# Writing a decode block's output in two halves: two column tiles, one PSUM bank, one copy and one eight-row transfer each

## The chip, the cores and the metric

The kernel runs on one core of one Trainium2 chip. The metric is the device time of one execution in microseconds (us), as the median of several runs. One further execution was taken with the profiler; its rows are what is read here.

## What is computed

One token for each of four sequences (B = 4, D = 512) passes a layer norm. The normalised row feeds an attention block and a gated feed-forward block, and both results are added to the row itself:

```python
xn = _layernorm(x)                                  # x: [4, 1, 512] bf16
q  = xn @ wq                                        # 32 heads of 128
k, v = the last W = 4096 positions of the caches    # 8 key/value heads, 4 query heads to each
a  = softmax(q k^T * 128**-0.5) v                   # per head
A  = a.reshape(4, 1, 4096) @ wo                     # [4096, 512]
Bf = (silu(xn @ w_gate) * (xn @ w_up)) @ w_down     # F = 1792
out = x + A + Bf                                    # [4, 1, 512] bf16
```

All inputs and the output are bf16. The output has four rows of 512 elements, 1 KB each.

## The kernel before

**Staging.** All large loads are put on SP's queue in one order: `wq`, `w_gate`, `w_up`, then keys and values of the eight key/value heads (4 MB each, two buffers each), `w_down`, and at the end `wo` in four pieces of 22, 5, 3 and 2 of its 32 row blocks (`WOS`, `load_wo`, line 257). `wo` takes the place of a key buffer. Loads of keys and values wait for the buffer to come free (`s_tr`, `s_pv`).

**Main loop.** For each of the eight heads TensorE (PE) transposes the keys, VectorE (DVE) and ScalarE (ACT) copy the transposes out of PSUM, PE forms the scores, DVE takes maxima, ACT the exponentials, and PE multiplies by the values. GpSimd (POOL) only builds constants at the start: memsets, then selections that write identity-like patterns, two semaphores (`s_go`, `s_const`) between them.

**The end, around the change.** The normalised attention output of the last head is permuted by PE into `perm_ps`, and DVE writes it to `OP` (line 374), of whose 32 columns per row block four (one per sequence) hold data and the rest are zero. `guT`, the feed-forward's hidden row, has the same layout (line 368). Two accumulators collect the output:

- `acc4` (line 478): one product of 32 x 512 for each row block, in bank `ps_S[1]`. Row block t goes to column tile t % 4 of the array, so that the four tiles hold four partial sums of the full 512 columns, at partitions 0, 32, 64 and 96. It takes all of `w_down` (14 blocks) and the first 22 blocks of `wo`.
- `acc` (line 482): for each row block four products of 4 x 128, one for each quarter of the output columns, quarter n in column tile n. All four lie in bank `ps_S[0]`, quarter n at partitions 32n to 32n+3. It starts with `x` itself (through an identity) and takes the last ten blocks of `wo`.

When `acc4` is complete (`s_e`), ACT copies it to `S2` in SBUF (line 292), and four fp32 products with the selector `sel4` add its four partial sums into `acc`, between the second and the third piece of `wo`. The last two blocks of `wo` wait for its fourth piece (`d_wo[3]`); the last product of all signals `s_acc`.

**The output.** On `s_acc` DVE copies quarters 0 and 1 from PSUM to `y` (line 377, two copies of 4 x 128), and ACT quarters 2 and 3 (line 295, two copies). `y` is a tile of 4 partitions x 512. Each half of the columns then goes out in one transfer of four rows of 512 bytes: the first on SP's queue (line 269, on `s_y[0]`), the second on ACT's (line 298, on `s_y[1]`). SP ends the kernel when both have landed (`d_out` at 32).

Of the kernel before, what the change touches and what calls it, by code (L numbers as in the profile page):

```python
# [3 lines left out]
BF16 = mybir.dt.bfloat16  # L4
FP32 = mybir.dt.float32
# [5 lines left out]
def bass_parallel_sum__sliding_block_cached__swiglu_ffn__decode_kernel(  # L11
# [39 lines left out]
    def sb(name, shape, dtype, align=32):  # L51
        return nc.alloc_sbuf_tensor(name, shape, dtype, align_bytes=align)
# [33 lines left out]
    on = sb("on", [128, NH], FP32)  # L86
    OT = sb("oT", [128, B, HKV, REP, 4], BF16)

    OP = sb("oP", [128, NR, 32], BF16)
    S2 = sb("s2", [128, D], FP32)  # L90
    sel4 = sb("sel4", [128, B], FP32)
    ex = sb("ex", [128, NF, B], FP32)
    gs = sb("gs", [128, NF, B], FP32)
    guT = sb("guT", [128, NF, 32], BF16)
# [8 lines left out]
    dr = sb("dr", [128, NR], BF16)  # L103
    sel = sb("sel", [128, 32], FP32)
    head = sb("head", [128, 128], FP32)
    y = sb("y_sb", [B, D], BF16)

    ps = nc.alloc_psum_tensor
    ps_kt = [ps("ps_kt%d" % s, [128, 512], FP32) for s in range(3)]
# [14 lines left out]
    up_ps = ps_O[:, 128:128 + NF * B]  # L124
    xT_ps = ps_S[2][:, 0:NC * B]
    HD = D // 4
    acc_ps = ps_S[0][:, 0:HD]
    acc4_ps = ps_S[1]
    perm_ps = ps_kt[2][:, 0:B * NR]

# [42 lines left out]
    s_y = [sem("s_y%d" % n) for n in range(2)]  # L173

    x_ap = A_x.rearrange("b s d -> (b s) d")
    out_ap = out.rearrange("b s (n c) -> n (b s) c", n=2)
    wq_ap = A_wq.rearrange("(p c) n -> p c n", c=NC)
    wg_ap = B_w_gate.rearrange("(p c) n -> p c n", c=NC)
    wu_ap = B_w_up.rearrange("(p c) n -> p c n", c=NC)
# [6 lines left out]
    def on_gpsimd(eng):  # L186
        eng.memset(ident[:], 0.0)
        eng.memset(I4[:], 0.0)
        eng.memset(ones[:], 1.0)
        eng.memset(own[:], 1.0)  # L190
        eng.memset(moff[:], 0.0)
        eng.memset(coff[:], 0.0)
        eng.memset(neg[:], 0.0)
        eng.memset(dq[:], 1.0)
        eng.memset(dr[:], 0.0)
        eng.memset(sel4[:], 0.0)
        eng.memset(guT[:].rearrange("p t b -> p (t b)"), 0.0)
        eng.memset(OP[:].rearrange("p t b -> p (t b)"), 0.0)
        eng.memset(sel[:], 0.0)
        eng.memset(head[:], 0.0)  # L200
        eng.memset(CM[:], 0.0)
        eng.memset(QT[:, HKV, :], 0.0)
        eng.drain().then_inc(s_go, 1)

        def select(t, pattern, op, fill, base, mult):
            eng.affine_select(t, t, pattern=pattern, compare_op=op, fill=fill, base=base,
                              channel_multiplier=mult)
        select(I4[:], [[-1, B]], ALU.not_equal, 1.0, 0, 1)
        select(ident[:], [[-1, 128]], ALU.not_equal, 1.0, 0, 1)
        select(neg[:], [[-1, NH]], ALU.not_equal, -1.0, 0, 1)  # L210
        ownv = own[:].rearrange("k (j b) -> k j b", b=B)
        moffv = moff[:].rearrange("k (j b) -> k j b", b=B)
        coffv = coff[:].rearrange("k (b h) -> k b h", h=REP)
        select(ownv, [[0, NJ], [-REP, B]], ALU.is_ge, 0.0, 0, 1)
        select(moffv, [[0, NJ], [-REP, B]], ALU.is_ge, OFF, 0, 1)
        select(coffv, [[-REP, B], [0, REP]], ALU.is_ge, OFF, 0, 1)
        select(dq[:], [[-32, 4]], ALU.is_ge, 0.0, 0, 1)
        select(dr[:], [[-1, NR]], ALU.not_equal, 1.0, 0, 1)
        eng.drain()
        select(ownv, [[0, NJ], [REP, B]], ALU.is_ge, 0.0, REP - 1, -1)  # L220
        select(moffv, [[0, NJ], [REP, B]], ALU.is_ge, OFF, REP - 1, -1)
        select(coffv, [[REP, B], [0, REP]], ALU.is_ge, OFF, REP - 1, -1)
        select(dq[:], [[32, 4]], ALU.is_ge, 0.0, 31, -1)
        for a in range(1, 4):
            eng.drain()
            select(dr[:], [[-1, NR]], ALU.not_equal, 1.0, -32 * a, 1)
        eng.drain().then_inc(s_const, 1)

        for n in range(4):
            select(sel[:], [[-1, 32]], ALU.not_equal, 1.0, -32 * n, 1)  # L230
            select(head[:], [[0, 128]], ALU.not_equal, 1.0, -32 * n, 1)
            select(sel4[:], [[-1, B]], ALU.not_equal, 1.0, -32 * n, 1)
            eng.drain()
        eng.memset(dsum[:], 0.0)
        eng.memset(Osb[:], 0.0)
        eng.drain().then_inc(s_zero, 1)

    def on_sync(eng):
        def load(g):
            u = g % 2  # L240
            if g >= 2:
                eng.wait_ge(s_tr, NCH * (g - 1))
            if g < HKV - 1:
                eng.dma_start(KB[u][:], kv_ap(A_k_cache, g, 0, NT)).then_inc(d_k[u], 16)
            else:

                H = NT // 2
                eng.dma_start(KB[u][:, 0:H], kv_ap(A_k_cache, g, 0, H)).then_inc(d_k[u], 16)
                eng.dma_start(KB[u][:, H:], kv_ap(A_k_cache, g, H, NT)).then_inc(d_kh, 16)
            if g == 1:  # L250
                eng.wait_ge(s_q, 1)
            if g >= 2:
                eng.wait_ge(s_pv, g - 1)
            eng.dma_start(VB[u], kv_ap(A_v_cache, g, 0, NT)).then_inc(d_v[u], 16)

        def load_wo(n, a, b):
            eng.dma_start(WO[:, a:b, :], wo_ap[:, a:b, :]).then_inc(d_wo[n], 16)  # L257

        eng.dma_start(WQ, wq_ap).then_inc(d_wq, 16)
        eng.dma_start(WG[:], wg_ap).then_inc(d_wg, 16)  # L260
        eng.dma_start(WU[:], wu_ap).then_inc(d_wu, 16)
        for g in range(HKV):
            load(g)
        eng.dma_start(WD[:], wd_ap).then_inc(d_wd, 16)
        eng.wait_ge(s_tr, NCH * (HKV - 1))
        for q in range(4):
            load_wo(q, WOS[q], WOS[q + 1])
        eng.wait_ge(s_y[0], 1)
        eng.dma_start(out_ap[0], y[:, 0:D // 2]).then_inc(d_out, 16)
        eng.wait_ge(d_out, 32)  # L270

    def on_scalar(eng):
        eng.wait_ge(s_go, 1)
        eng.dma_start(X[:], x_ap).then_inc(d_x, 16)
        eng.wait_ge(s_var, 1)
        eng.activation(st_std[:], st_var[:], ACT.Sqrt).then_inc(s_std, 1)

        def group(r):
            for n, c in enumerate(ACT_CH):
                eng.wait_ge(s_tr, r * NCH + (c + 1))  # L280
                eng.activation(KT[:, c % 4], kt_ps[c % 3], ACT.Copy).then_inc(s_ea, 1)  # L281
            for q in range(NB):
                eng.wait_ge(s_mk, r * NB + (q + 1))
                eng.activation(P[:, BT * q:BT * (q + 1), :], ps_S[q][:].rearrange("p (t n) -> p t n", n=NH),  # L284
                               ACT.Exp, scale=SCALE).then_inc(s_p, 1)

        eng.wait_ge(s_gu, 1)
        eng.activation(ex[:], gate_ps.rearrange("p (t b) -> p t b", b=B), ACT.Exp, scale=-1.0).then_inc(s_ex, 1)
        with eng.Fori(0, HKV) as r:
            group(r)  # L290
        eng.wait_ge(s_e, 1)
        eng.activation(S2[:], acc4_ps[:], ACT.Copy).then_inc(s_ec, 1)
        eng.wait_ge(s_acc, 1)
        for n in range(2, 4):
            last = eng.activation(y[:, HD * n:HD * (n + 1)], acc_ps[32 * n:32 * n + B, :], ACT.Copy)
        last.then_inc(s_y[1], 1)
        eng.wait_ge(s_y[1], 1)
        eng.dma_start(out_ap[1], y[:, D // 2:D]).then_inc(d_out, 16)

    def on_vector(eng):  # L300
        eng.wait_ge(d_x, 16)
# [63 lines left out]
        eng.drain()  # L365
        eng.tensor_tensor(gs[:], gate_ps.rearrange("p (t b) -> p t b", b=B), ex[:], ALU.mult)
        eng.drain()
        eng.tensor_tensor(guT[:, :, 0:B], up_ps.rearrange("p (t b) -> p t b", b=B), gs[:], ALU.mult).then_inc(s_guT, 1)
        group(0)
        with eng.Fori(1, HKV) as r:  # L370
            group(r, lambda: norm(r - 1))
        norm(HKV - 1)
        eng.wait_ge(s_pm, 1)
        eng.tensor_copy(OP[:, :, 0:B].rearrange("p r b -> p b r"), perm_ps.rearrange("p (b r) -> p b r", b=B)).then_inc(s_pc, 1)
        eng.wait_ge(s_acc, 1)
        for n in range(2):
            last = eng.tensor_copy(y[:, HD * n:HD * (n + 1)], acc_ps[32 * n:32 * n + B, :])  # L377
        last.then_inc(s_y[0], 1)

    def on_tensor(eng):  # L380
        mm = eng.matmul
# [95 lines left out]
        def acc4(n, left, right, start, stop):  # L477
            return mm(acc4_ps[32 * n:32 * n + 32, :], left, right, start=start, stop=stop, skip_group_check=True)

        def acc(left, right, start, stop):  # L480
            for n in range(4):
                last = mm(acc_ps[32 * n:32 * n + B, :], left, right[:, HD * n:HD * (n + 1)],
                          start=start, stop=stop, skip_group_check=True)
            return last

# [38 lines left out]
            last = mm(perm_ps[:, NR * b:NR * (b + 1)], OT[:, b].rearrange("p k h q -> p (k h q)"), dr[:])  # L524
        last.then_inc(s_pm, 1)
        spin(2, 1)
        acc(ident[0:B, 0:B], X[:], True, False)
        eng.wait_ge(s_pc, 1)
        for q in range(4):
            eng.wait_ge(d_wo[q], 16)  # L530
            for e in range(WOS[q], WOS[q + 1]):
                if e < WOE:
                    last = acc4(e % 4, OP[:, e, :], WO[:, e, :], False, e >= WOE - 4)
                else:
                    last = acc(OP[:, e, 0:B], WO[:, e, :], False, e == NR - 1)
            if WOS[q + 1] == WOE:
                last.then_inc(s_e, 1)
            if q == 1:
                eng.wait_ge(s_ec, 1)
                acc(sel4[:], S2[:], False, False)  # L540
        last.then_inc(s_acc, 1)

# [33 lines left out]
```

## Time and profile before

| | before |
|---|---|
| median of 3 runs | 195.66 us (195.49 to 195.70) |
| the profiled execution's own time | 195.57 us |
| its span, first to last instruction | 194.2 us |
| granted TensorE clock, mean | 0.991 |
| busy: PE, DVE, ACT, POOL | 158.9, 103.5, 61.6, 10.2 us |
| HBM read | 81.01 MB, 417 GB/s over the span |

The span is 1.37 us shorter than that execution's time. Times inside the profile count from the start of the span. In a list of instructions in order of time a row gives the start, the time from the first start to the last end, the engine, the line, what it writes and reads, and how many instructions were merged. SPq and ACTq are the queues of SyncE and ScalarE on which transfers are issued; the duration there is that of issuing, not of the transfer. PEld is the loading of weights into TensorE.

### The profile page before, as it was taken

What the parts mean: (1) busy time and instruction counts of PE and PEld (TensorE: products, weight loads), DVE (VectorE), ACT (ScalarE), POOL (GpSimd) and SP (SyncE); (2) the same over time, 40 slices, a digit from 0 to 9 for tenths busy, and PEclk for the clock granted to TensorE, in tenths of its full rate; (3) what the DMA queues carried; (4) which work ended last, traced back from release to release, by engine and by line L of the source; (5) the groups of instructions that cost most, each with busy time, mean ns of one, the idle gap of its engine ahead of it and who ended that gap; (6) DMA issues with size and microseconds to landing.
All of it is one profiled execution on the core that took longest, in us unless ns stands there. A gap on an engine that the chain in (4) does not pass through costs nothing.

```text
span 194.2 us, 7226 instructions
## 1 busy us (share of the span) xinstructions
PE 158.9 (82%) x3138; PEld 131.4 (68%) x3138; DVE 103.5 (53%) x218; ACT 61.6 (32%) x79; POOL 10.2 (5%) x49
## 2 busy tenths in 40 slices
PE   0009843998699899999999899989996999999964
PEld 0009843997388849966994699459945984897531
DVE  0071020368256837871886389338933893678241
ACT  1020000243405442624451345314531553063402
POOL 8750000000000000000000000000000000000000
PEclk9999999999789999999999999999999999999999
DMA  6999999999999999999999999999999999999992
GB/s 216 433 436 428 430 429 432 432 429 432 429 439 430 422 429 459 432 432 439 432 439 432 432 432 439 432 439 432 432 432 432 432 402 432 462 439 399 440 398 104
DMA packets 3634, 81.16 MB, mean 418 GB/s; under 512 B 412, under 2 KB 424, under 8 KB 808
## 3 DMA queue, kind: packets, MB, share of 16 engines
q1 hardware_dynamic: 3608, 81.01, 97.3%
q8 instruction: 8, 0.13, 0.2%
q14 instruction: 2, 0.02, 0.0%
q10 hardware_dynamic: 16, 0.01, 0.0%
HBM read 81.01 MB, written 0.00 MB: 417 GB/s over the span
## 4 chain that ended last, share of the span: by engine, by line
DMA 59%; PE 35%; DVE 3%; SPq 1%; issue 1%; DVEq 0%
DMA kbuf<-in_A_k_cache_dram 43%; PE ps_kt L417 21%; DMA kbuf<-in_A_wo_dram 16%; PE ps_s L432 7%; PE ps_o L453 3%; PE ps_s L468 1%; PE ps_kt L474 1%; PE ps_s L444 1%; DVE kT L330 1%; DVE mx L336 1%; SPq L257 1%; PE ps_s L466 1%; PE ps_o L459 0%; DVE y_sb L377 0%; PE ps_kt L439 0%
## 5 line engine op out<-in xcount | busy, mean ns | idle before, releaser
L417 PE MATMUL ps_kt<-ident,kbuf 128*128 128x128 bf16 x1024 | 78.4, 224 | 10.2 <-DMA kbuf<-in_A_k_cache_dram 9.8
L417 PEld LDWEIGHTS ps_kt<-ident,kbuf 128*128 128x128 bf16 x1024 | 60.7, 100 | 12.2 <-DMA kbuf<-in_A_k_cache_dram 10.9
L330 DVE COPY kT<-ps_kt 128x1024 bf16<-128x1024 bf16 x88 | 57.7, 686 | 20.4 <-PE ps_kt L417 19.6
L281 ACT ACTIVATE kT<-ps_kt 128x1024 bf16<-128x1024 bf16 x40 | 41.0, 1024 | 65.4 <-PE ps_kt L417 65.4
L432 PE MATMUL ps_s<-qC,kT 128*128 128x16 bf16 x1024 | 44.9, 170 | 2.9 <-DVE kT L330 2.0
L432 PEld LDWEIGHTS ps_s<-qC,kT 128*128 128x128 bf16 x1024 | 38.0, 97 | 4.8 <-DVE kT L330 4.0
L284 ACT ACTIVATE p<-ps_s 128x512 bf16<-128x512 f32 x32 | 16.5, 602 | 34.3 <-PE ps_s L444 34.3
L336 DVE TENSOR_REDUCE mx<-ps_s 128x16 f32<-128x512 f32 x32 | 22.0, 689 | 6.2 <-PE ps_s L432 4.2
L474 PE MATMUL ps_kt<-own,ones 128*128 128x512 bf16 x84 | 21.2, 380 | 0.0
L453 PE MATMUL ps_o<-vbuf,p 128*32 128x256 bf16 x512 | 19.2, 290 | 0.3
L453 PEld LDWEIGHTS ps_o<-vbuf,p 128*32 128x32 bf16 x512 | 15.0, 102 | 6.0 <-ACT p L284 4.2
L348 DVE COPY osb<-ps_o 128x256 f32<-128x256 f32 x8 | 3.4, 425 | 28.7 <-PE ps_o L459 28.7
L459 PE MATMUL ps_o<-p,ones 128*32 128x256 bf16 x64 | 16.9, 288 | 0.0
L385 PE MATMUL ps_s<-i,xn 4*128 4x4 f32 x4 | 0.6, 254 | 14.5 <-DVE xn L316 14.5
L474 PEld LDWEIGHTS ps_kt<-own,ones 128*128 128x128 bf16 x84 | 6.8, 97 | 6.8 <-issue 0.6
L385 PEld LDWEIGHTS ps_s<-i,xn 4*128 4x128 f32 x4 | 0.5, 207 | 14.4 <-issue 14.4
L444 PE MATMUL ps_s<-cm,own 128*128 128x512 bf16 x32 | 8.3, 380 | 1.0 <-DVE cm L345 1.0
L459 PEld LDWEIGHTS ps_o<-p,ones 128*32 128x32 bf16 x64 | 6.6, 103 | 0.1
L302 DVE TENSOR_REDUCE st_sum<-x_sb 4x1 f32<-4x512 bf16 x1 | 0.7, 674 | 10.2 <-DMA x_sb<-in_A_x_dram 10.2
L444 PEld LDWEIGHTS ps_s<-cm,own 128*128 128x128 bf16 x32 | 2.5, 97 | 5.3 <-DVE cm L345 3.4
L468 PE MATMUL ps_s<-sel,osb 128*128 128x16 f32 x36 | 5.8, 275 | 0.0
L468 PEld LDWEIGHTS ps_s<-sel,osb 128*128 128x128 f32 x36 | 5.2, 208 | 0.0
(85 smaller groups left out, 76.1 us busy)
## 6 DMA issues: line engine op xcount, KB each, us to landing
vbuf<-in_A_v_cache_dram SPq DMA_DIRECT2D x8, 4096.0 KB, 30.3
kbuf<-in_A_k_cache_dram SPq DMA_DIRECT2D x7, 4096.0 KB, 27.0
vbuf<-in_A_wq_dram SPq DMA_DIRECT2D x1, 4096.0 KB, 12.1
kbuf<-in_A_k_cache_dram SPq DMA_DIRECT2D x2, 2048.0 KB, 25.3
kbuf<-in_A_wo_dram SPq DMA_DIRECT2D x1, 2816.0 KB, 29.4
wg_sb<-in_B_w_gate_dram SPq DMA_DIRECT2D x1, 1792.0 KB, 16.2
wu_sb<-in_B_w_up_dram SPq DMA_DIRECT2D x1, 1792.0 KB, 21.1
wd_sb<-in_B_w_down_dram SPq DMA_DIRECT2D x1, 1792.0 KB, 34.5
```

What stands on the lines that cost most here:

```text
L281: eng.activation(KT[:, c % 4], kt_ps[c % 3], ACT.Copy).then_inc(s_ea, 1)
L284: eng.activation(P[:, BT * q:BT * (q + 1), :], ps_S[q][:].rearrange("p (t n) -> p t n", n=NH), ACT.Exp, scale=SCALE).then_inc(s_p, 1)
L330: eng.tensor_copy(KT[:, c % 4], kt_ps[c % 3]).then_inc(s_ev, 1)
L336: eng.tensor_reduce(mx[:, q, :], ps_S[q][:].rearrange("p (t n) -> p n t", n=NH), AX.X, ALU.max)
L348: eng.tensor_copy(Osb[:], O_ps)
L417: last = eng.transpose(kt_ps[c % 3][:, k, :], KB[u][:, CH * c + k, :], ident[:])
L432: last = mm(ps_S[q][:, NH * t:NH * (t + 1)], KT[:, c % 4, k, :], QC[:], start=(t == 0), stop=False, skip_group_check=True)
L444: mm(ps_S[q][:].rearrange("p (t n) -> p t n", n=NH), own[:], CM[:].unsqueeze(1).to_broadcast([128, BT, NH]), start=False, stop=True, skip_ ...
L453: mm(O_ps[32 * n:32 * n + 32, :], P[:, t:t + 2, :].rearrange("p t n -> p (t n)"), VB[u][:, t:t + 2, :].rearrange("p t d -> p (t d)"), star ...
L459: last = mm(den_ps[32 * n:32 * n + 32, :], ones[:, 0:32], P[:, DT * e:DT * (e + 1), :].rearrange("p t n -> p (t n)"), start=False, stop=(e ...
L468: last = mm(O2_ps, Osb[:, Dh * h:Dh * (h + 1)], sel[:, NH * h:NH * (h + 1)], start=(h == 0), stop=(h == 1), skip_group_check=True)
L474: mm(ps_kt[k][:], ones[:], own[:].unsqueeze(1).to_broadcast([128, 4, 128]), skip_group_check=True)
```

## The change

The output keeps its four column quarters in four column tiles, but in two halves. Quarters 0 and 1 accumulate in bank `ps_S[0]`, quarters 2 and 3 in bank `ps_S[2]`.

- In each quarter the four sequences stand eight partitions apart (0, 8, 16, 24 of the tile's 32), not side by side. For that `OP` and `guT` get their data in columns 0, 8, 16 and 24, `x` enters through a new selector `I8` (4 x 32, a one at row p, column 8p), and the products of `acc` are 32 rows wide, not 4. `sel4` is gone; the existing `sel` (128 x 32) takes its place.
- `y` is 128 partitions x 128 columns. DVE copies the first half in one instruction of 64 x 128 and ACT the second in one of 64 x 128.
- Each half goes out in one transfer of eight rows of 256 bytes: every eighth partition of the half of `y`, to two quarters x four sequences in DRAM.
- The products on the fourth piece of `wo` are ordered by halves: both row blocks of quarters 0 and 1, a signal, both row blocks of quarters 2 and 3, a signal. DVE waits for the first, ACT for both.
- POOL makes one selection more before `s_const` (`I8`) and four fewer after it (`sel4`).

```diff
-    sel4 = sb("sel4", [128, B], FP32)
+    I8 = sb("i8", [B, 32], BF16)
...
-    y = sb("y_sb", [B, D], BF16)
+    y = sb("y_sb", [128, D // 4], BF16)
...
-    acc_ps = ps_S[0][:, 0:HD]
+    acc_ps = [ps_S[2 * h][:, 0:HD] for h in range(2)]
...
-    out_ap = out.rearrange("b s (n c) -> n (b s) c", n=2)
+    out_ap = out.rearrange("b s (n c) -> n (b s) c", n=4)
...
+        select(I8[:], [[-1, 32]], ALU.not_equal, 1.0, 0, 8)
...
-            select(sel4[:], [[-1, B]], ALU.not_equal, 1.0, -32 * n, 1)
...
         eng.wait_ge(s_y[0], 1)
-        eng.dma_start(out_ap[0], y[:, 0:D // 2]).then_inc(d_out, 16)
+        eng.dma_start(out_ap[0:2], y[0:64:8]).then_inc(d_out, 16)
...
-        eng.wait_ge(s_acc, 1)
-        for n in range(2, 4):
-            last = eng.activation(y[:, HD * n:HD * (n + 1)], acc_ps[32 * n:32 * n + B, :], ACT.Copy)
-        last.then_inc(s_y[1], 1)
+        eng.wait_ge(s_acc, 2)
+        eng.activation(y[64:128], acc_ps[1][64:128], ACT.Copy).then_inc(s_y[1], 1)
         eng.wait_ge(s_y[1], 1)
-        eng.dma_start(out_ap[1], y[:, D // 2:D]).then_inc(d_out, 16)
+        eng.dma_start(out_ap[2:4], y[64:128:8]).then_inc(d_out, 16)
...
-        eng.tensor_tensor(guT[:, :, 0:B], up_ps.rearrange("p (t b) -> p t b", b=B), gs[:], ALU.mult).then_inc(s_guT, 1)
+        eng.tensor_tensor(guT[:, :, 0:32:8], up_ps.rearrange("p (t b) -> p t b", b=B), gs[:], ALU.mult).then_inc(s_guT, 1)
...
-        eng.tensor_copy(OP[:, :, 0:B].rearrange("p r b -> p b r"), perm_ps.rearrange("p (b r) -> p b r", b=B)).then_inc(s_pc, 1)
+        eng.tensor_copy(OP[:, :, 0:32:8].rearrange("p r b -> p b r"), perm_ps.rearrange("p (b r) -> p b r", b=B)).then_inc(s_pc, 1)
         eng.wait_ge(s_acc, 1)
-        for n in range(2):
-            last = eng.tensor_copy(y[:, HD * n:HD * (n + 1)], acc_ps[32 * n:32 * n + B, :])
-        last.then_inc(s_y[0], 1)
+        eng.tensor_copy(y[0:64], acc_ps[0][0:64]).then_inc(s_y[0], 1)
...
-        def acc(left, right, start, stop):
-            for n in range(4):
-                last = mm(acc_ps[32 * n:32 * n + B, :], left, right[:, HD * n:HD * (n + 1)],
+        def acc(left, right, start, stop, tiles=range(4)):
+            for n in tiles:
+                last = mm(acc_ps[n // 2][32 * n:32 * n + 32, :], left, right[:, HD * n:HD * (n + 1)],
                           start=start, stop=stop, skip_group_check=True)
...
-        acc(ident[0:B, 0:B], X[:], True, False)
+        acc(I8[:], X[:], True, False)
         eng.wait_ge(s_pc, 1)
-        for q in range(4):
+        for q in range(3):
...
-                    last = acc(OP[:, e, 0:B], WO[:, e, :], False, e == NR - 1)
+                    acc(OP[:, e, :], WO[:, e, :], False, False)
...
-                acc(sel4[:], S2[:], False, False)
-        last.then_inc(s_acc, 1)
+                acc(sel[:], S2[:], False, False)
+        eng.wait_ge(d_wo[3], 16)
+        for h in range(2):
+            for e in range(WOS[3], NR):
+                last = acc(OP[:, e, :], WO[:, e, :], False, e == NR - 1, (2 * h, 2 * h + 1))
+            last.then_inc(s_acc, 1)
```

More of the change, by code (lines that the diff above doesn't have):

```diff
@@ L195, in on_gpsimd @@
         eng.memset(dr[:], 0.0)
-        eng.memset(sel4[:], 0.0)
+        eng.memset(I8[:], 0.0)
         eng.memset(guT[:].rearrange("p t b -> p (t b)"), 0.0)
```

## The prediction

> **What bounds the kernel now.** I read the page first, for the whole span and the chain of work that ended last.
>
> ```profile
> span 194.2 us, 7226 instructions
> ...
> DMA  6999999999999999999999999999999999999992
> ...
> DMA 59%; PE 35%; DVE 3%; SPq 1%; issue 1%; DVEq 0%
> ```
>
> The transfer engines are full in 38 of 40 slices. The loads set the pace until the last piece of `wo` is in, and the change touches no load. So only what follows that landing can move the end. The chain in order of time names that stretch:
>
> ```profile
> 160.67 31.17 DMA kbuf<-in_A_wo_dram
> ...
> 191.89 0.31 PE ps_s L482 x8
> ...
> 192.23 0.28 DVE y_sb L377
> ...
> 192.52 0.28 DVE y_sb L377
> ```
>
> The wait for `wo` ends at 191.85. Eight products and DVE's two copies follow. The instructions in order of time show that both halves of the output run side by side:
>
> ```profile
> 191.27 0.35 PE L482 MATMUL ps_s<-kbuf,oP 128*4 128x128 bf16 x12
> 191.89 0.28 PE L482 MATMUL ps_s<-kbuf,oP 128*4 128x128 bf16 x8 [0.27 <-DMA kbuf<-in_A_wo_dram]
> 192.22 0.55 ACT L295 ACTIVATE y_sb<-ps_s 4x128 bf16<-4x128 f32 x2 [1.22 <-PE ps_s L482]
> 192.23 0.57 DVE L377 CAST y_sb<-ps_s 4x128 bf16<-4x128 f32 x2 [4.04 <-PE ps_s L482]
> 192.81 0.27 ACTq L298 DMA_DIRECT2D out_dram<-y_sb  x1
> 192.83 0.35 SPq L269 DMA_DIRECT2D out_dram<-y_sb  x1
> ```
>
> The view of the DMA queues, narrowed to 0.10 us, shows each transfer's packets one by one. A column is 2.5 ns. First ACT's transfer, from 193.56 to 193.66:
>
> ```profile
> GB/s 0 0 0 0 205 0 0 0 0 0 0 0 206 0 0 0 0 0 0 205 2 0 0 0 0 0 0 0 206 0 0 0 0 0 0 0 0 2 0 0
> DMA packets 8, 0.00 MB, mean 21 GB/s; under 512 B 4, under 2 KB 8, under 8 KB 8
> q10 hardware_dynamic: 8, 0.00, 8.6%
> ```
>
> Then SP's, from 193.66 to 193.76, and after it nothing until the span's end:
>
> ```profile
> GB/s 0 0 0 0 205 0 0 0 0 0 0 0 206 0 0 0 0 0 0 205 2 0 0 0 0 0 0 0 206 0 0 0 0 0 0 0 0 2 0 0
> DMA packets 8, 0.00 MB, mean 21 GB/s; under 512 B 4, under 2 KB 8, under 8 KB 8
> q1 hardware_dynamic: 8, 0.00, 8.6%
> ```
>
> Four rows of 512 bytes go out some 0.02 us apart, and four small packets (the counts on the semaphore) close them. ACT's first row starts at 193.57, which is 0.49 after its issue ended (192.81 + 0.27). SP's starts at 193.67, also 0.49 after its issue ended (192.83 + 0.35). SP's last packet is at 193.75, and 0.43 later the span ends at 194.18. So the tail is: products 0.31, copies 0.57, issue 0.35, 0.49 to the first row, 0.08 of rows, 0.43 to the end. SP's half is the later one, by 0.10.
>
> **Copies.** One copy of 64 x 128 takes the place of two of 4 x 128 on each engine. The rows, with minimum, median and maximum in ns:
>
> ```profile
> L295 ACT ACTIVATE y_sb<-ps_s x2: 270/271/272, 192.2 to 192.5; 4x128 bf16<-4x128 f32 x2
> ```
>
> ```profile
> L377 DVE CAST y_sb<-ps_s x2: 278/280/281, 192.2 to 192.5; 4x128 bf16<-4x128 f32 x2
> ```
>
> ```profile
> L320 DVE CAST qT<-ps_s x1: 292/292/292, 18.9 to 18.9; 128x128 bf16<-128x128 f32 x1
> ```
>
> The last row is a cast of the same 128 elements from PSUM on 128 partitions, at 0.29. So 64 partitions cost DVE what 4 do, 0.28, and I take ACT's 0.27 unchanged too. Gone are 0.29 on DVE (192.80 to 192.51) and 0.27 on ACT.
>
> **Products.** They keep their number and get 32 rows in place of 4. The rows for the rate:
>
> ```profile
> 180.21 1.25 PE L474 MATMUL ps_kt<-own,ones 128*128 128x512 bf16 x5
> ...
> 188.90 1.47 PE L478 MATMUL ps_s<-kbuf,oP 128*32 128x512 bf16 x22 [0.86 <-DMA kbuf<-in_A_wo_dram]
> 190.34 0.45 PE L482 MATMUL ps_s<-kbuf,oP 128*4 128x128 bf16 x20
> ```
>
> One product of 512 columns on the whole array takes (1.25 - 0.38) / 4 = 0.218 of streaming, with 0.38 for a single one, so 128 columns take 0.054. Spread over four column tiles, 512 columns at 32 rows start every (1.47 - 0.38) / 21 = 0.052, a quarter of 0.218: the tiles run at once, and 32 rows of weights are no brake. 128 columns at 4 rows start every (0.45 - 0.22) / 19 = 0.012. At 32 rows I take a quarter of 0.052, 0.013. The bounds are 0.012 and, if the wider weights should hold back the short products, twice that; for the last eight that is at most 0.1.
>
> The new order gives up half of the concurrency in the last piece. Quarters 0 and 1 need two rounds of 0.054, so the first half's last product starts 0.06 after the first. That is where the last of eight starts now (0.28 - 0.22). DVE's start stays at 192.23. Quarters 2 and 3 then need another round, and ACT starts 0.07 later, at 192.29. Putting the first half first therefore brings DVE nothing by itself, and costs ACT 0.07.
>
> **Issue of the transfers.** Here the change pays. Now both sides of a transfer are plain: four rows against four partitions. Afterwards DRAM has quarters times sequences, with steps that do not merge into one, against eight partitions. The key loads have that form (blocks times sequences against 128 partitions), the `wo` loads the plain one:
>
> ```profile
> L244 SPq DMA_DIRECT2D kbuf<-in_A_k_cache_dram x7: 534/535/657, 2.2 to 120.7; - x7
> ```
>
> ```profile
> L257 SPq DMA_DIRECT2D kbuf<-in_A_wo_dram x4: 334/434/434, 159.3 to 160.7; - x4
> ```
>
> ```profile
> L298 ACTq DMA_DIRECT2D out_dram<-y_sb x1: 274/274/274, 192.8 to 192.8; - x1
> ```
>
> ```profile
> L269 SPq DMA_DIRECT2D out_dram<-y_sb x1: 348/348/348, 192.8 to 192.8; - x1
> ```
>
> ```profile
> L274 ACTq DMA_DIRECT2D x_sb<-in_A_x_dram x1: 628/628/628, 3.3 to 3.3; - x1
> ```
>
> A plain transfer issued with none ahead of it takes 0.334 (the first of `wo`, 128 rows) or 0.348 (the output, 4 rows), so the number of rows does not matter. One with the additional dimension takes 0.535. I add the difference, 0.19, to both queues. Bounds: nothing, if the dimension is free for so small a transfer; 0.31 on SP from the longest key load (0.657), and 0.35 on ACT from `x`'s load (0.628 against 0.274). I take 0.19 because seven key loads have a median that stands beside their minimum.
>
> **Rows.** Eight rows 0.02 apart take 0.14 to the last one's start where four take 0.06: 0.08 more. That they are of 256 bytes I cost at nothing, since small packets close each transfer now at the same pace. The upper bound is one further round to memory for each, for which the nearest number is the 0.43 between the last packet and the end.
>
> **The rest** is covered:
>
> ```profile
> 187.47 0.72 DVE L374 CAST oP<-ps_kt 128x128 bf16<-128x128 f32 x1 [0.36 <-PE ps_kt L524]
> 188.87 1.01 PEld L478 LDWEIGHTS ps_s<-kbuf,oP 128*32 128x32 bf16 x22 [0.97 <-DVE oP L374]
> ```
>
> ```profile
> 8.00 0.21 POOL L206 TENSOR_SCALAR_AFFINE_SELECT dr<-dr 128x32 bf16<-128x32 bf16 x1 [0.19 <-issue]
> ...
> 14.46 0.61 PE L385 MATMUL ps_s<-i,xn 4*128 4x4 f32 x4 [14.46 <-DVE xn L316]
> ...
> 27.78 0.22 DVE L368 TENSOR_TENSOR guT<-ps_o,gs 128x56 bf16<-128x56 f32 x1
> 32.53 0.56 PEld L417 LDWEIGHTS ps_kt<-ident,kbuf 128*128 128x128 bf16 x6 [6.25 <-DMA kbuf<-in_A_k_cache_dram]
> ```
>
> `OP` is written with another step, in the same 128 x 128 form. It ends at 188.19, and PE then waits for `wo` until 188.87, so 0.68 hide any slowdown. `guT` ends at 28.00, 4.5 before PE's keys. The selection that POOL makes ahead of `s_const` (0.21) moves its last one's end from 8.21 to 8.42, while PE waits for `xn` until 14.46. The last product ahead of the fourth piece starts at 191.40 (191.27 + 0.35 - 0.22), 0.49 before the next can: the 40 wider products of the pieces before (8 of them on `S2`) take 0.04 more at 0.013 each, and 0.5 at the upper bound. Without these covers each would count in full. ACT's longer wait (two signals) has only its own transfer behind it; DVE's has nothing.
>
> **The sum.** SP: copy ends 192.51, issue from 192.54 (0.03 after it, as now) to 193.08, first row 193.57, last packet 193.57 + 0.14 + 0.02 = 193.73. Now it is 193.75. ACT: copy 192.29 to 192.56, issue from 192.60 to 193.06, first row 193.55, last packet 193.71. SP's stays the later one, and the end moves by 0.02. The profiled execution would take 195.57 - 0.02 = 195.55. It stands 0.09 under the median, so the median becomes 195.64.
>
> [...]
>
> **Rivals.** *The issue does not grow.* The key loads may take longer for another reason, their 4 MB. Then SP's last packet comes 0.21 earlier (0.29 less 0.08), ACT's at 193.52, and the median is 195.45. For it: output and first `wo` load agree in spite of 128 rows against 4. Against it: `wo`'s first piece is large as well, with 2,816 KB, and issues in 0.334.
>
> [...]
>
> *More than the sum: faster.* SP's rows follow ACT's without a gap, so the two may be generated in turn. If SP's transfer, ready first, no longer stood behind ACT's, 0.10 more would go, with 0.21 a gain of 0.31: 195.35. To be faster by over 0.39 even that needs something that no row shows.
>
> **Chances.** 0.2% of the median is 0.39 us, about what a measurement of this kernel can tell from no change. Forecast with the longer issue 0.55, issue unchanged 0.20, small rows 0.18, more than the sum 0.07. The first two lie within 0.39: same 0.75. Slower 0.18. I count the last as faster, 0.07, though its priced part stays inside. The forecast's own range is 195.45 (no growth) to 195.80 (the upper issue bounds, +0.10 and +0.13 on the end). The whole range goes down to 195.3, which is the faster rival, and up to 196.2, which takes in the small rows just past their deciding point; their dear end is left out.
>
> **What would show it.** Right: one copy of 0.28 and one of 0.27; SP's starting at about the same distance from the last landing, ACT's 0.07 later; both issues at 0.46 to 0.54; eight rows within some 0.16; the end 0.43 after the last packet. The forecast is wrong if the issues stay at 0.27 and 0.35 (then it is faster by 0.2), if the rows are spread over more than 0.3 us or the wait from the last row to the end grows (small rows), if the products of the last piece take longer than 0.35, or if the last piece of `wo` lands at another distance from the start than 191.85, which none of the steps explains.

## The result: 195.85 us, slower by 0.28 us

| | before | after |
|---|---|---|
| median | 195.57 us (22 runs) | 195.85 us (22 runs) |
| lowest, highest | 195.40, 195.73 | 195.72, 196.04 |
| the profiled execution's own time | 195.57 | 195.85 |
| its span | 194.2 | 194.6 |

The ratio after to before is 1.0016, with a 95% interval from 1.0009 to 1.0022. The ratio is inside the 0.2% of the forecast's "same", but clear of no change, and on the other side of the predicted 0.02 gain.

The instructions of the changed kernel's end in order of time (start, length, engine, line, what it does):

```profile
191.99 0.30 PE L480 MATMUL ps_s<-kbuf,oP 128*32 128x128 bf16 x8 [0.25 <-DMA kbuf<-in_A_wo_dram]
192.32 0.28 DVE L376 CAST y_sb<-ps_s 64x128 bf16<-64x128 f32 x1 [4.00 <-PE ps_s L480]
192.38 0.27 ACT L296 ACTIVATE y_sb<-ps_s 64x128 bf16<-64x128 f32 x1 [1.31 <-PE ps_s L480]
192.63 0.67 SPq L271 DMA_DIRECT2D out_dram<-y_sb  x1
192.68 0.62 ACTq L298 DMA_DIRECT2D out_dram<-y_sb  x1
```

The first product of the last piece of `wo` starts 0.10 later than in the profile before (191.99 against 191.89), because that piece landed 0.10 later (191.95 against 191.85), one of the prediction's signs of being wrong. But over the profiles of all kernels run here that start lies between 191.89 and 192.12, on both sides of the change alike. So I do not take it for an effect of the change, and count everything from it. Copies and products are as forecast: one copy of 0.28 and one of 0.27, DVE's 0.33 after the first product, ACT's 0.39. The issues are not: 0.67 on SP and 0.62 on ACT, where the forecast had 0.54 and 0.46.

The packets of the two transfers, from the view of the DMA queues (2.5 ns a column). SP's queue, from 193.90 to 194.00:

```profile
GB/s 0 102 0 0 102 102 0 0 0 102 0 102 0 0 0 102 0 102 0 0 102 0 2 0 0 0 2 0 0 0 0 0 0 0 0 0 0 0 0 0
DMA packets 10, 0.00 MB, mean 21 GB/s; under 512 B 10, under 2 KB 10, under 8 KB 10
q1 hardware_dynamic: 10, 0.00, 9.6%
```

ACT's queue, from 194.15 to 194.25:

```profile
GB/s 0 0 0 0 0 0 0 0 102 0 0 0 102 102 0 0 102 0 0 102 0 0 102 0 102 0 0 0 102 0 2 0 0 2 0 0 0 0 0 0
q10 hardware_dynamic: 10, 0.00, 9.5%
```

The eight rows start within 0.05 (four rows before: 0.06), so the rows themselves cost nothing. But SP's first row comes 0.60 after its issue ended (193.90 against 193.30, where it was 0.49), and ACT's comes 0.87 after its own (194.17 against 193.30), 0.27 behind SP's. Each transfer has two small closing packets (10 packets, eight of them rows), where each had four before (8 packets, four of them rows). How many engines carried a transfer no trace here shows; where an expectation counts engines, the traces have the closing packets.

Counted from the first product, SP's first row moved from 1.78 to 1.91: copies 0.30 earlier, issue 0.32 longer, 0.11 more from the issue's end to the row. ACT's rows then follow 0.27 behind it, where before SP's stood 0.10 behind ACT's and was the last. The last packet moves from 1.86 to 2.24, by 0.38. The span ends 0.46 after it before and 0.37 now. So from the first product to the end of the span it is 2.33 before and 2.62 now, 0.29 more, beside 0.28 between the medians.

### The profile page after: what moved, and what is told of

The parts are those of the page before. It is cut to its first block, busy times and chain, and to the rows that moved or that the text cites. A ratio compares the mean times of both kernels' runs of the same rounds, so it can differ in the third digit from the quotient of the medians.

```text
span 194.6 us, 7218 instructions
## 1 busy us (share of the span) xinstructions
PE 158.8 (82%) x3138; PEld 131.2 (67%) x3138; DVE 103.5 (53%) x217; ACT 61.4 (32%) x78; POOL 9.0 (5%) x46
## 4 chain that ended last, share of the span: by engine, by line
DMA 59%; PE 35%; DVE 2%; SPq 1%; issue 1%; ACT 0%; DVEq 0%
DMA kbuf<-in_A_k_cache_dram 43%; PE ps_kt L415 21%; DMA kbuf<-in_A_wo_dram 16%; PE ps_s L430 7%; PE ps_o L451 3%; PE ps_s L466 1%; PE ps_kt L472 1%; PE ps_s L442 1%; DVE kT L330 1%; SPq L259 1%; PE ps_s L464 1%; PE ps_o L457 0%; DVE mx L336 0%; PE ps_kt L437 0%; SPq L263 0%
```

## Experiments

So the question was what makes the issue long and the rows late. The theory at first was **form**: the second DRAM dimension. (The form of a transfer is how many dimensions and which steps its two sides have.) Its rivals were **rows** (eight, or 256 bytes), **two queues** (issued 0.05 apart), and later **partition step** (eight partitions apart). All times have the kernel before beside them at 195.57 to 195.59.

**The DRAM form undone, rows one after another (plain_rows).**

```diff
-    out_ap = out.rearrange("b s (n c) -> n (b s) c", n=4)
+    out_ap = out.rearrange("b s (n c) -> (b s n) c", n=4)
...
-        eng.dma_start(out_ap[0:2], y[0:64:8]).then_inc(d_out, 16)
+        eng.dma_start(out_ap[0:8], y[0:64:8]).then_inc(d_out, 16)
...
-        eng.dma_start(out_ap[2:4], y[64:128:8]).then_inc(d_out, 16)
+        eng.dma_start(out_ap[8:16], y[64:128:8]).then_inc(d_out, 16)
```

> The changed kernel with the form of its two output transfers alone undone: each half's eight rows of 256 bytes go to eight successive rows of 256 bytes in DRAM, one dimension in place of two (the output's blocks stand in another order). Theory form: it is the additional DRAM dimension that costs, so the issues fall from 0.67 and 0.62 to about 0.35 and 0.27, the first row comes 0.49 after the issue, SP's half comes 0.21 earlier than in the kernel before, and the time is about 195.36 (0.2 under before). Theory rows: eight rows of 256 bytes cost by themselves, so the time stays at 195.85 (0.28 over before). Theory two queues: the two issues now start 0.05 apart and slow each other; the issues stay long and the time stays at 195.85.

Measured 195.94, ratio 1.0021 (1.0012 to 1.0030). The issues, from the view of the output tensor (minimum, median, maximum in ns):

```profile
L271 SPq DMA_DIRECT2D out_dram<-y_sb x1: 714/714/714, 192.6 to 192.6; - x1
L298 ACTq DMA_DIRECT2D out_dram<-y_sb x1: 669/669/669, 192.7 to 192.7; - x1
```

The DRAM dimension is gone and nothing got shorter. The theory that named it as the only cause here fell.

**The form alone, on the kernel before (form_only).**

```diff
-    out_ap = out.rearrange("b s (n c) -> n (b s) c", n=2)
+    out_ap = out.rearrange("(u v) s (n c) -> n v (u s) c", n=2, v=2)
```

> The kernel before with the form alone added: four rows of 512 bytes as before, but to two DRAM dimensions of 2 and 2 (rows 1 and 2 of the output are exchanged). Theory form: issues of about 0.67 and 0.62, 0.60 from the issue's end to the first row, the second transfer's rows 0.27 behind the first's, so the last packet comes 0.6 later and the time is about 196.2. Theory rows: four rows of 512 bytes, so as before, 195.57. Theory two queues: the issues start 0.02 apart as before, 195.57.

Measured 196.36, ratio 1.0040 (1.0026 to 1.0054):

```profile
L298 ACTq DMA_DIRECT2D out_dram<-y_sb x1: 725/725/725, 193.0 to 193.0; - x1
L269 SPq DMA_DIRECT2D out_dram<-y_sb x1: 767/767/767, 193.1 to 193.1; - x1
```

Rows, partitions and copies are those of before; the second dimension is enough by itself for the long issue. So the changed kernel, whose issue stays long without it, must have a second reason as well.

**The form on both sides (form_k4).** The kernel before with eight rows of 256 bytes in each transfer, from its four partitions, so that both sides have a further dimension.

```diff
+    y_h = y[:].rearrange("b (m n c) -> b n m c", m=2, n=2)
-    out_ap = out.rearrange("b s (n c) -> n (b s) c", n=2)
+    out_ap = out.rearrange("b s (m n c) -> n (b s) m c", m=2, n=2)
-        eng.dma_start(out_ap[0], y[:, 0:D // 2]).then_inc(d_out, 16)
+        eng.dma_start(out_ap[0], y_h[:, 0]).then_inc(d_out, 16)
```

(ACT's likewise; DVE copies quarters 0 and 2, ACT 1 and 3.)

> [...] Theory form, if it is the dimension: long issues and about 196.2. [...] Theory rows: 0.28 more than before, 195.85, with short issues.

Measured 196.35, ratio 1.0039 (1.0025 to 1.0052):

```profile
L299 ACTq DMA_DIRECT2D out_dram<-y_sb x1: 761/761/761, 192.9 to 192.9; - x1
L270 SPq DMA_DIRECT2D out_dram<-y_sb x1: 827/827/827, 192.9 to 192.9; - x1
```

Here the further dimension stands on both sides, and each queue has four closing packets (12 packets, eight of them rows) where form_only has two (6 packets, four of them rows). The issues are long all the same, 0.76 and 0.83 against 0.73 and 0.77, so it is the dimension, not the number of closing packets.

**One of the two transfers (act_only).**

```diff
         eng.wait_ge(s_y[0], 1)
-        eng.dma_start(out_ap[0:2], y[0:64:8]).then_inc(d_out, 16)
-        eng.wait_ge(d_out, 32)
+        eng.wait_ge(d_out, 16)
```

> The changed kernel without SP's transfer: the first half of the output is not written, ACT's transfer of the second half is as it is. If the two transfers are made ready one after the other, ACT's first row comes 0.60 after its issue and not 0.87, and the time is about 195.58 (0.27 under the changed kernel). If the two issues also slow each other, ACT's issue falls as well, to 0.46 (0.27 + 0.19 of the prediction) or less, and the time to about 195.4. If each transfer has its delay by itself, issue 0.62 and 0.87 stay and the time stays at 195.85.

Measured 195.71, ratio to before 1.0006 (0.9997 to 1.0015). The issue, from the instructions in order of time, and the packets from 194.00 to 194.15 (3.75 ns a column):

```profile
192.78 0.62 ACTq L297 DMA_DIRECT2D out_dram<-y_sb  x1
```

```profile
GB/s 0 0 0 0 0 0 0 0 0 0 0 0 0 68 0 0 137 0 0 68 0 68 0 68 68 0 68 0 1 0 1 0 0 0 0 0 0 0 0 0
```

With no other output transfer the issue is as long, 0.62, so two queues are not its cause. But the first row, at 194.05, comes 0.65 after the issue and not 0.87: in the changed kernel ACT's rows came 0.22 later because of SP's transfer. Counted from the first product (192.09 here) the last packet comes 0.22 earlier, at 2.02. The median fell by 0.14 where 0.27 was expected; intervals of this width do not settle that amount.

**Every second block of DRAM (plain_stride).** As plain_rows, with one step of 512 bytes instead of a merged run.

```diff
-    out_ap = out.rearrange("b s (n c) -> n (b s) c", n=4)
+    out_ap = out.rearrange("b s (m n c) -> n (b s m) c", m=2, n=2)
...
-        eng.dma_start(out_ap[0:2], y[0:64:8]).then_inc(d_out, 16)
+        eng.dma_start(out_ap[0], y[0:64:8]).then_inc(d_out, 16)
...
-        eng.dma_start(out_ap[2:4], y[64:128:8]).then_inc(d_out, 16)
+        eng.dma_start(out_ap[1], y[64:128:8]).then_inc(d_out, 16)
```

> As the changed kernel, but each half's eight rows of 256 bytes go to every second block of 256 bytes in DRAM: one uniform step, eight rows against eight partitions, and not one merged run of 2 KB as in the run before (the output's blocks stand in another order). Theory mismatch (an issue is short only where both sides have the same two dimensions; a DRAM side that merges into one run, as x's load has it, or that has one more, is long): issues of 0.35 and 0.27, time about 195.36. Theory small rows (256 bytes, or partitions eight apart): issues stay at 0.67 and 0.71, 195.9. Theory row count (another number of rows or engines than four): long too, 195.9.

Measured 195.91, ratio 1.0016 (1.0007 to 1.0025):

```profile
L271 SPq DMA_DIRECT2D out_dram<-y_sb x1: 715/715/715, 192.8 to 192.8; - x1
L298 ACTq DMA_DIRECT2D out_dram<-y_sb x1: 669/669/669, 192.8 to 192.8; - x1
```

A merged run in DRAM is not it either.

**Four plain transfers (four_plain).**

```diff
-        eng.dma_start(out_ap[0:2], y[0:64:8]).then_inc(d_out, 16)
+        for n in range(2):
+            eng.dma_start(out_ap[n], y[32 * n:32 * n + 32:8]).then_inc(d_out, 16)
```

(ACT's likewise, with n = 2 and 3.)

> As the changed kernel, but each quarter goes out in a plain transfer of its own: four rows of 256 bytes from partitions eight apart, DRAM step 1 KB, two transfers on each queue. Theory mismatch and theory row count: first issues 0.35 and 0.27, second ones about 0.43, last packet 0.18 later than in the kernel before, 195.75. Theory small rows: each issue about 0.62, the second ends 0.6 later than that, 196.4.

Measured 196.74, ratio 1.0065 (1.0051 to 1.0079):

```profile
L272 SPq DMA_DIRECT2D out_dram<-y_sb x2: 640/692/745, 192.6 to 193.4; - x2
L300 ACTq DMA_DIRECT2D out_dram<-y_sb x2: 694/700/707, 192.6 to 193.4; - x2
```

Four rows, one DRAM step, four closing packets to a transfer, and still 0.64 to 0.75 each. The second of a queue is long too (0.64 on SP, 0.69 or 0.71 on ACT), so it is not the first use of a form. Left were the 256 bytes and the partitions eight apart.

**One transfer (one_transfer).** The kernel before; after all four copies ACT sends four rows of 1 KB, SP nothing.

```diff
-        eng.dma_start(out_ap[1], y[:, D // 2:D]).then_inc(d_out, 16)
+        eng.wait_ge(s_y[0], 1)
+        eng.dma_start(out.rearrange("b s d -> (b s) d"), y[:]).then_inc(d_out, 16)
```

> The kernel before with one output transfer in place of two: four rows of 1 KB on ACT's queue after all four copies; in DRAM they are one run of 4 KB. Theory mismatch: the run merges as for x's load, issue about 0.62 and 0.60 to the first row, 195.97. Theory small rows and theory row count: issue 0.27, first row 0.49 after it, last packet 0.06 earlier than before, 195.5.

Measured 195.50, ratio 0.9996 (0.9987 to 1.0005):

```profile
L297 ACTq DMA_DIRECT2D out_dram<-y_sb x1: 274/274/274, 193.1 to 193.1; - x1
```

Short, though DRAM is one run. Theory mismatch was wrong here as well. `x`'s load has this form in the other direction and issues in 0.63, so the form alone does not explain that one.

**The partition step alone (step8).** The changed kernel's products and order, with two copies on each engine and rows of 512 bytes.

```diff
-        eng.dma_start(out_ap[0:2], y[0:64:8]).then_inc(d_out, 16)
+        eng.dma_start(out_ap[0], y[0:32:8, 0:D // 2]).then_inc(d_out, 16)
-        eng.tensor_copy(y[0:64], acc_ps[0][0:64]).then_inc(s_y[0], 1)
+        for n in range(2):
+            last = eng.tensor_copy(y[:, HD * n:HD * (n + 1)], acc_ps[0][32 * n:32 * n + 32, :])
+        last.then_inc(s_y[0], 1)
```

> The changed kernel's products, order and 32-row tiles, but two copies on each engine (32 x 128) and transfers of four rows of 512 bytes to DRAM as in the kernel before; only that the four partitions are eight apart. Theory partition step (an issue is short only from adjacent partitions): issues of about 0.7, the second transfer's rows 0.27 behind the first's, about 196.35 as with the form alone. Theory small rows (256 bytes make the long issue in the four plain transfers): issues 0.35 and 0.27, time 195.57 to 195.65, ACT's copies 0.06 later.

Measured 196.34, ratio 1.0041 (1.0028 to 1.0055):

```profile
L271 SPq DMA_DIRECT2D out_dram<-y_sb x1: 745/745/745, 192.8 to 192.8; - x1
L300 ACTq DMA_DIRECT2D out_dram<-y_sb x1: 689/689/689, 192.9 to 192.9; - x1
```

**The small rows alone (rows256).** The kernel before with four transfers of four rows of 256 bytes from adjacent partitions.

```diff
-        eng.dma_start(out_ap[0], y[:, 0:D // 2]).then_inc(d_out, 16)
+        for n in range(2):
+            eng.dma_start(out_ap[n], y[:, HD * n:HD * (n + 1)]).then_inc(d_out, 16)
```

> The kernel before with four plain transfers: each quarter's four rows of 256 bytes from adjacent partitions, two transfers on each queue. Theory small rows: each issue about 0.7, as in the four plain transfers of the changed kernel, but 0.29 later: about 197.0. Theory partition step: issues of 0.35 and 0.43 on SP, last packet 0.47 later than before, about 196.05.

Measured 195.89, ratio 1.0017 (1.0008 to 1.0026):

```profile
L300 ACTq DMA_DIRECT2D out_dram<-y_sb x2: 272/293/314, 192.8 to 193.1; - x2
L270 SPq DMA_DIRECT2D out_dram<-y_sb x2: 303/326/348, 192.9 to 193.3; - x2
```

These two runs decide: four rows of the old size from partitions eight apart are long, four small rows from adjacent ones are short. The slower time of rows256 fits its two further issues: SP's second one ends 0.39 later than the only one before (193.56 against 193.17). The rows themselves show no cost of being small: the four of each transfer start within 0.06, as the rows of 512 bytes do.

**A step of two (step2).**

```diff
-        eng.dma_start(out_ap[0], y[0:32:8, 0:D // 2]).then_inc(d_out, 16)
+        eng.dma_start(out_ap[0], y[0:8:2, 0:D // 2]).then_inc(d_out, 16)
```

(Against step8; `OP`, `guT` and `I8` place the sequences two apart.)

> As the run with two copies and four rows of 512 bytes from partitions eight apart, but two apart. If any step other than one makes the issue long: 0.7 and 196.3, as with eight. If it grows with the step: issues between 0.35 and 0.7, 195.7 to 196.0.

Measured 196.31, ratio 1.0036 (1.0023 to 1.0050):

```profile
L271 SPq DMA_DIRECT2D out_dram<-y_sb x1: 749/749/749, 192.8 to 192.8; - x1
L300 ACTq DMA_DIRECT2D out_dram<-y_sb x1: 694/694/694, 192.9 to 192.9; - x1
```

It does not grow with the step: two costs what eight does, 0.75 and 0.69 in both. So the form that is cheap at issue here has adjacent partitions and one step in DRAM.

**The change in the cheap form (adjacent).**

```diff
-    out_ap = out.rearrange("b s (n c) -> n (b s) c", n=4)
+    out_ap = out.rearrange("b s (m n c) -> n (b s m) c", m=2, n=2)
-        eng.dma_start(out_ap[0:2], y[0:64:8]).then_inc(d_out, 16)
+        eng.dma_start(out_ap[0], y[0:8]).then_inc(d_out, 16)
-                last = mm(acc_ps[n // 2][32 * n:32 * n + 32, :], left, right[:, HD * n:HD * (n + 1)],
+                mm(acc_ps[h][32 * h:32 * h + 8, :], left[:, 1 - m:9 - m], right[:, HD * n:HD * (n + 1)],
```

(n = 2m + h; `OP` and `guT` hold the sequences in columns 1, 3, 5, 7, and the slice of 8 columns that starts at 1 - m sets their place.)

> The change with its transfers put into the cheap form: half h is quarters h and h+2, both in column tile h, sequence b of the m-th of them at partition 2b+m, so that a half's eight rows of 256 bytes come from eight adjacent partitions and go to DRAM at one step of 512 bytes. One copy of 8 x 128 for each half. Price: each half's products on the last piece run one after another in one tile, last start 0.11 later. Theory partition step: issues 0.35 and 0.27, copies ready 0.18 earlier than in the kernel before, time about 195.39. If eight rows (or eight engines) are long at issue by themselves: 0.7 each, about 195.95.

Measured 195.53 beside 195.59 before, ratio 0.9995 (0.9986 to 1.0004). Products, weight loads and issues in order of time, and both queues' packets from 193.50 to 193.65:

```profile
191.44 0.94 PE L483 MATMUL ps_s<-kbuf,oP 128*8 128x128 bf16 x20
192.00 0.21 PEld L483 LDWEIGHTS ps_s<-kbuf,oP 128*8 128x8 bf16 x8 [0.23 <-DMA kbuf<-in_A_wo_dram]
192.42 0.28 DVE L376 CAST y_sb<-ps_s 8x128 bf16<-8x128 f32 x1 [4.25 <-PE ps_s L483]
192.46 0.27 ACT L296 ACTIVATE y_sb<-ps_s 8x128 bf16<-8x128 f32 x1 [1.51 <-PE ps_s L483]
192.73 0.37 SPq L271 DMA_DIRECT2D out_dram<-y_sb  x1
192.75 0.30 ACTq L298 DMA_DIRECT2D out_dram<-y_sb  x1
```

```profile
GB/s 0 0 0 0 0 0 0 137 0 0 139 68 0 0 139 0 68 1 2 137 1 68 138 1 1 70 68 0 1 1 68 0 0 1 0 0 0 0 0 0
q10 hardware_dynamic: 16, 0.00, 8.0%
q1 hardware_dynamic: 16, 0.00, 7.9%
```

Eight rows of 256 bytes, with eight closing packets on each queue, issue in 0.37 and 0.30, and the rows of both queues interleave: the 0.27 between the queues is gone too. This takes back the loss. Of the expected gain of 0.18 only 0.06 is measured, and the interval includes no change. The products are not what is missing. The twenty of the last two pieces stand in one row, but the weight loads of the last eight waited 0.23 for `wo`, and the first of these products starts at 192.00. From there SP's issue starts after 0.73 (0.94 before), and the last packet, at 193.63, comes after 1.63 (1.86 before): 0.23 earlier. But the span then ends 0.58 after the last packet, where it was 0.46, so that from the first product on it is only 0.12 shorter. What delays that end is open.

**Crossed copies on the kernel before (crossed).**

```diff
-        for n in range(2):
-            last = eng.tensor_copy(y[:, HD * n:HD * (n + 1)], acc_ps[32 * n:32 * n + B, :])
-        last.then_inc(s_y[0], 1)
+        for n in (0, 2):
+            eng.tensor_copy(y[:, HD * n:HD * (n + 1)], acc_ps[32 * n:32 * n + B, :]).then_inc(s_y[0], 1)
```

(ACT copies 1 and 3; SP waits for one copy of each engine, ACT's transfer for two.)

> The kernel before with the copies crossed: DVE copies quarters 0 and 2, ACT 1 and 3, so that the first half is in SBUF after one copy of each engine and SP's transfer, of the form of before, goes out 0.29 earlier; ACT's goes at its time. All theories: SP's issue 0.35 from 0.65 after the first product of the last piece (192.54 where that starts at 191.89), ACT's unchanged; ACT's transfer is then the last, 0.10 before SP's of now, 195.47. If the gap of 0.10 between the two transfers' rows was no queue but SP's longer issue alone, the same.

Measured 195.45, ratio 0.9996 (0.9987 to 1.0005), near the expected 195.47, but the interval includes no change:

```profile
192.27 0.59 DVE L378 CAST y_sb<-ps_s 4x128 bf16<-4x128 f32 x2 [4.00 <-PE ps_s L482]
192.62 0.35 SPq L270 DMA_DIRECT2D out_dram<-y_sb  x1
192.95 0.27 ACTq L299 DMA_DIRECT2D out_dram<-y_sb  x1
```

SP's issue starts 0.69 after the first product (0.94 before). Its first row, at 193.40, comes 0.43 after the issue ended, where it was 0.49: where ACT's transfer comes later, SP's rows are out 0.06 sooner. No kernel run here is shown to be faster than the one before.

## Why the prediction was wrong

Term by term, on the way to the end of the span: copies -0.30 (forecast -0.29), issue +0.32 (+0.19), from the issue to SP's first row +0.11 (nothing), rows -0.02 (+0.08), ACT's rows behind SP's +0.27 (nothing), from the last packet to the end -0.09 (nothing). That is +0.29, where the forecast came to -0.02.

- **Copies, products, order, covers: right.** One copy takes 0.28 or 0.27 on 64 partitions. The last eight products take 0.30 (0.28 before). Doing the first half first brings DVE nothing (0.33 after the first product, 0.34 before) and costs ACT 0.06 (0.39 against 0.33 for its first copy, forecast 0.07). `OP` is written in 0.71 (0.72 before), and PE still waits 0.79 for `wo` ahead of the products that read it.
- **Issue: the term that was mis-sized.** 0.19 was taken for both queues, from the DRAM dimension and the median of the key loads. It measured 0.32 on SP and 0.35 on ACT. The prediction also saw only one of the two causes. Partitions eight apart, which it passed over, are enough for the long issue (step8), as the DRAM dimension is (form_only, where it added 0.42 and 0.45 and not 0.19). That the forecast's upper bounds, 0.31 and 0.35, came out nearly right is luck: the first was taken from one key load near the start, while the later ones of the same form take 0.53 or 0.54, the second from `x`'s load, whose form issues in 0.27 as a store (one_transfer).
- **From the issue to the rows: the step that failed outright.** 0.49 was kept for both queues as if it did not depend on the form. It became 0.60 on SP and 0.87 on ACT. Without SP's transfer ACT's is 0.65 (act_only), so 0.22 of its 0.38 comes from the other transfer. So SP's half was not the last, as the sum had it, but ACT's, 0.27 behind. The prediction had asked whether the two transfers are made ready in turn, but only as a gain of 0.10 in a rival; the sum carried no such delay into the new form.
- **Rows: 0.08 was added and nothing was needed.** From the first row to the last closing packet it is 0.06, against 0.08 for four rows. The upper bound, a further round to memory for each row, was the author's estimate from the 0.43 at the end; no run shows such a round.
- **The rivals.** No run shows small rows that wait for one another, to which the chances gave 0.18 and the range its end at 196.2: eight start within 0.05 in the changed kernel, four within 0.05 to 0.06 in rows256. The slower result came from the forecast's own mechanism: its upper issue bounds gave 195.80, a loss of 0.14, and the delay behind the issue made it 0.28. That the issue does not grow was wrong, and among the signs against the forecast none was an issue longer than 0.54.
- **Slips that change nothing.** 194.18 is where the last count on the semaphore lands; the span ends at 194.22. ACT's upper bound moves the end by 0.12 (193.71 + 0.16 against 193.75), not 0.13.

## What to carry to other kernels

When a kernel ends in a small transfer, its issue can take longer than a copy that feeds it (0.35 against 0.28 here, and 0.67 in the long form). Before re-laying the data for a cheaper copy, read the issue row of a transfer of the same form, on both sides. Here one copy less saved 0.29, and the transfer's new form cost 0.32 at issue, 0.11 to the first row, and 0.27 by which one queue's rows trailed the other's. The cheaper copy did not need that form: adjacent has one copy for each half as well, and lost nothing, though no gain is shown for it either. Of the forms run here, keep adjacent partitions and one step in DRAM for such a transfer.

## What the runs showed of the hardware

- The issue of an output transfer took 0.27 to 0.37 from adjacent partitions with one step in DRAM, whether of four rows or eight, of 256 bytes, 512 or 1 KB. It took 0.62 to 0.83 from partitions two or eight apart, or with a further dimension. Why is open; the two together (0.67 and 0.62) are not longer than one alone (0.71 and 0.67 in plain_rows, 0.77 and 0.73 in form_only). `x`'s load, plain on both sides, took 0.63, which stays unexplained.
- In the long form the second queue's rows came 0.27 behind the first's (changed kernel). In the cheap form they came 0.10 behind in the kernel before and interleaved in adjacent. What holds them back was not tested beyond leaving one transfer out (act_only) and sending one earlier (crossed).
- Rows of 256 bytes went out at the pace of rows of 512: four start within 0.05 to 0.06 in rows256, within 0.06 in the kernel before.
